# A pair's one-hot rows transposed straight to their places, query casts off GpSimd, later weight slots and a split last tile, in a new hand-written order

## The chip, the cores and the metric

The kernel runs on one core of one Trainium2 chip. The time is device microseconds of one execution. The kernel before was timed three times: 864.74, 865.45 and 865.73 us, median 865.45 us. The engines are named here as the profile names them: PE (TensorE, with PEld for its weight loads), DVE (VectorE), ACT (ScalarE), POOL (GpSimd) and SP (SyncE, which here only issues transfers).

## The reference

Three stages follow one another. The first is attention in which a query sees only the keys of its own cluster, for 2 batches, 8 heads, 768 positions and 64 channels, with 16 clusters; then come two feed-forward blocks.

```python
q_assign = argmax(q_n @ c_n.T)          # one of 16 clusters for each query
k_assign = argmax(k_n @ c_n.T)
mask   = q_assign[:, None] == k_assign[None, :]
scores = where(mask, 0.125 * q @ k.T, -1e9)
x      = softmax(scores) @ v            # heads side by side: 1536 tokens x 512
h = x @ w_in                            # 512 -> 2048
x = where(h > 0, h, exp(min(h, 0)) - 1) @ w_out
return ((x @ w_a) * (x @ w_b)) @ w_out2 # 512 -> 1536 -> 512
```

## The kernel before

Heads are worked off in 8 pairs, each with two halves of three tiles of 128 queries (tile numbers 0 to 5). Every float32 operand is carried as a high part and the rest, so that a product is two or three matmuls. The whole program is one list of words in a string, ORDER, such as `sc:9.4`. A word names a small function and its numbers, and each engine carries out its instructions in the order in which the list issues them. No scheduler moves them.

The words that matter here are these. `lk`, `lq` and `vl` load keys, queries and values. `ka1`, `ka2` and `kbd` make the two parts of the keys; `qa` and `qb` make those of the scaled queries. A third number, where there is one, picks the engine (0 DVE, 1 ACT, 2 POOL). `sm` multiplies a pair with the centroids, `sv`, `st` and `m1` to `m5` turn that into a one-hot row of 16 per head (`oht`). `oh` transposes it on PE for four rows sets at once (two heads, queries and keys), `ohs` scales it on ACT (query rows to 0 or -2^100, key rows to 1 or 0), and `ohd` moves the four pieces by DMA into partitions 64 to 79 of `qb` and `kb`. So the second matmul of a score tile (`sc`, L649, K of 80) adds the mask. `rm` is the negated row maximum on DVE, `ex` the exponential on ACT. Then nearly a third of the tiles (30 of 96) is split into two float16 parts (`hi` on ACT or POOL, `lo` on POOL) and transposed by DMA (`td`); the others are transposed on PE (`tr`) and split from PSUM (`th`, `tl`). `av` is the product with the values, whose parts are `v1` and `v2`; `ra`, `rc`, `rx`, `rb`, `re` and `ev` divide by the row sums.

`wm` issues 8 matmuls on zeros to a scratch bank; the list has 60 of them, all before the second pair's scores. `c0` to `c4` prepare the centroids, with one PE transpose in `c3` (L358).

A weight block of 512 columns comes as int64 pairs that hold float64 (`wl`, 512 KB), and `wa`, `w0` to `w4`, `wh`, `ws` and `wq` turn it into two float32 parts. The block's slot is taken from its pool in `wa` (L829). The feed-forward blocks follow with `h`, `x2`, `ab` and `o`; `oa` adds an `o` tile to the result and, in the last block, sends it out. `o:2.2.1` is the last of them: both its token tiles share one PSUM tile, and `oa` adds and sends them one after the other (L1042 to L1048).

Of the kernel before, what the change touches and what calls it, by code (L numbers as in the profile page):

```python
# [21 lines left out]
P = 128  # L22
# [40 lines left out]

ORDER = """
lk:1.1 wm:0 wm:2 cs:0 cz:0 lq:0.0 ib:0 wm:3 wm:5 lk:0.0 wm:8 lq:1.1 wm:11 vl:0 wm:12 vl:1 md:0 wm:15
kb:1 c0:0 vl:2 wm:18 wm:13 c1:0 vl:3 ka1:1.1 mo:0 c2:0 sb:0 wm:19 wl:0 wm:14 qa:0.2 ce:0 c3:0 wm:28
c4:0 ka2:1.2 wm:29 wm:33 kb:0 wm:35 wm:34 ka1:0.1 qb:0 wm:30 lk:3.0 wm:41 ka2:0.0 wm:10 lq:2.0 wm:46
wm:45 qa:1.2 lk:2.0 wm:47 vr:2 wm:25 qb:1 wm:26 vr:0 wm:56 vr:3 lq:3.0 sm:0.0 vr:1 sm:0.1 sv:0.0.0
vr:5 vr:4 vr:6 wm:22 sv:0.1.0 vr:7 wm:16 st:0 vr:10 wm:38 vr:11 m1:0 wm:20 vr:8 m2:0 wm:40 vr:9 m3:0
wm:57 wm:42 m4:0 wm:48 m5:0 vr:15 wm:31 vr:13 oh:0 wm:55 ohs:0 wm:4 wm:50 wa:0 ohd:0 wm:53 ka1:3.0  # L70
wm:39 vr:12 w0:0 wm:27 vr:14 w1:0 wm:17 kbd:3 w2:0 qa:2.1 vtp:0 wm:43 w3:0 wm:21 wh:0 w4:0 wm:37
ka1:2.1 wm:52 vtd:0 ws:0 wm:58 qa:3.1 kbd:2 sc:0.0 wq:0 sc:0.1 rm:0.0 vbp:0 wm:24 rm:0.1 ka2:2.2
ex:0.0 wl:1 wm:7 wm:36 vbd:0 wm:6 ex:0.1 tr:0.0.0 qb:3 tr:0.0.1 th:0.0.0.1 sc:0.2 th:0.0.1.1 qb:2
tr:0.1.0 sc:1.0 th:0.1.0.1 rm:0.2 vs:0 lq:4.0 wm:1 vs:2 wa:1 rm:1.0 wm:44 lq:5.0 wm:23 ex:0.2
ka2:3.2 wm:32 tl:0.0.0 wm:9 tl:0.1.0 hi:0.2.1 tr:0.1.1 tl:0.0.1 sc:1.1 vs:3 ex:1.0 lk:4.0 sm:1.0
# [178 lines left out]
def clustered_attention_moe_kernel(  # L254
# [842 lines left out]
```

## Time and profile before

| what | value |
|---|---|
| median of 3 | 865.45 us |
| profiled execution | 868.19 us, its span 866.4 us |
| PE busy | 833.2 us (96% of the span) |
| DVE busy | 612.2 us (71%) |
| ACT busy | 412.1 us (48%) |
| POOL busy | 355.5 us (41%) |

The profiled execution is one run by itself, 2.74 us above the median, and 1.8 us of it lie outside its span. PE is busy nearly throughout, but this is an average over stages: in the feed-forward blocks it never waits, in the attention it does. A matmul's end is modelled, so a busy PE is not always a PE at its peak, and where PE's granted clock in the rows is 0.5 it takes twice as long for the same matmuls.

### The profile page before, as it was taken

Reading aid. Unit: us, or ns where it says so; the run is one execution under the profiler, and the core shown is the slowest. Engines: PE = TensorE matmul, PEld = TensorE weight load, DVE = VectorE, ACT = ScalarE, POOL = GpSimd, SP = SyncE. Lnnn points to the kernel's source line nnn. Section 1 sums busy time; section 2 is a strip of 40 time slices with the busy share of each in tenths; the row PEclk is TensorE's granted clock in tenths of the full one; section 3 lists DMA queues with packets and bytes.
Section 4 is the critical chain, followed back from the end, with each engine's and each line's share of the span. In section 5 each row is a group of like instructions: output and inputs, shape, how many; then the busy total and the mean of one; then the engine's idle time right before and its main releaser. Section 6 shows DMA issues by size and latency. Waiting matters only on the chain.

```text
span 866.4 us, 12164 instructions
## 1 busy us (share of the span) xinstructions
PE 833.2 (96%) x4608; PEld 667.4 (77%) x4608; DVE 612.2 (71%) x883; ACT 412.1 (48%) x732; POOL 355.5 (41%) x290
## 2 busy tenths in 40 slices
PE   9898899998898999999999999999999999999997
PEld 8876676676666888888888888888888888888886
DVE  5898898897688986777887876884257872684222
ACT  6587686875677764264264265432122421232120
POOL 4577657674824323444444543342015530451000
PEclk9998999998898999999999999999999999999999
DMA  9445636654323212222222321121002320220102
GB/s 278 111 105 118 137 57 120 135 131 76 74 47 80 67 53 70 97 74 83 88 73 74 91 81 48 54 94 49 0 25 98 96 75 1 74 73 1 49 1 97
DMA packets 65754, 68.32 MB, mean 79 GB/s; under 512 B 49952, under 2 KB 49952, under 8 KB 65696
## 3 DMA queue, kind: packets, MB, share of 16 engines
q1 hardware_dynamic: 65392, 66.86, 29.2%
q10 hardware_dynamic: 304, 0.69, 0.4%
q8 instruction: 36, 0.59, 0.3%
q14 instruction: 22, 0.18, 0.1%
HBM read 48.27 MB, written 3.15 MB: 59 GB/s over the span
## 4 chain that ended last, share of the span: by engine, by line
PE 85%; DVE 7%; POOL 3%; ACT 2%; issue 1%; DMA 0%; ACTq 0%; DVEq 0%; POOLq 0%
PE ab L900 8%; PE ab L901 8%; PE ab L902 8%; PE sc L649 5%; PE h L900 5%; PE h L901 5%; PE h L902 5%; PE x L900 5%; PE x L901 5%; PE x L902 5%; PE tt L701 4%; PE av L760 4%; PE o L902 4%; PE o L900 4%; PE o L901 4%; PE sm L569 3%
## 5 line engine op out<-in xcount | busy, mean ns | idle before, releaser
L657 DVE TENSOR_REDUCE nm<-sc 128x1 f32<-128x768 f32 x96 | 90.2, 948 | 19.9 <-PE sc L649 19.4
L668 ACT ACTIVATE pf<-sc,nm 128x768 f32<-128x768 f32 x96 | 86.5, 902 | 35.2 <-DVE nm L657 31.2
L1002 ACT COPY t0ab<-ab 128x512 f32<-128x512 f32 x36 | 21.1, 587 | 123.1 <-PE ab L902 123.1
L701 PE MATMUL tt<-identf,pf 128*128 128x128 f32 x396 | 65.1, 298 | 14.1 <-DVE pt L710 7.7
L1007 DVE TENSOR_TENSOR t1ab<-ab,t0ab 128x512 f32<-128x512 f32 x36 | 24.8, 688 | 73.2 <-ACT t0ab L1002 73.2
L710 DVE TENSOR_TENSOR pt<-tt,pt 128x384 f16<-128x384 f32 x132 | 68.7, 545 | 8.5 <-ACT pt L705 8.2
L701 PEld LDWEIGHTS tt<-identf,pf 128*128 128x128 f32 x396 | 49.6, 152 | 27.2 <-ACT pf L668 12.0
L649 PE MATMUL sc<-ka,qa 128*128 128x384 f32 x192 | 60.5, 398 | 9.8 <-ACT pf L668 9.8
L705 ACT CAST pt<-tt 128x384 f16<-128x384 f32 x126 | 57.0, 478 | 25.2 <-PE tt L701 24.1
L683 POOL TENSOR_TENSOR phl<-pf,phl 128x768 f16<-128x768 f32 x30 | 50.8, 1693 | 39.9 <-ACT phl L676 37.4
L760 PE MATMUL av<-pt,v 128*64 128x384 f16 x576 | 52.8, 329 | 0.0
L1018 DVE TENSOR_TENSOR gl<-t1ab,gh 128x512 fp32r<-128x512 f32 x36 | 38.4, 1065 | 19.9 <-ACT gh L1013 19.9
L649 PE MATMUL sc<-kb,qb 80*128 80x384 f32 x192 | 52.4, 356 | 0.0
L866 DVE SCALAR_TENSOR_TENSOR wg<-wraw,wg 128x512 f32<-128x512 uint32 x68 | 47.4, 698 | 2.3
L853 DVE SCALAR_TENSOR_TENSOR wf<-wraw,wg 128x512 int32<-128x512 int32 x68 | 47.0, 691 | 2.1
L956 DVE SCALAR_TENSOR_TENSOR t1h<-t0h,h 128x1024 f32<-128x1024 f32 x24 | 29.2, 1215 | 25.2 <-ACT t0h L951 25.1
L649 PEld LDWEIGHTS sc<-ka,qa 128*128 128x128 f32 x192 | 31.6, 203 | 18.9 <-ACT pf L668 13.6
L836 ACT ACTIVATE wg<-wraw 128x512 f32<-128x512 f32 x68 | 45.1, 667 | 1.6 <-DMA wraw<-in_w_a_dram 0.9
L760 PEld LDWEIGHTS <-v 128*64 128x64 f16 x576 | 31.3, 110 | 16.2 <-issue 4.9
L971 DVE TENSOR_TENSOR gl<-t1h,gh 128x1024 fp32r<-128x1024 f32 x24 | 36.1, 1504 | 5.4 <-ACT gh L964 5.4
L841 DVE TENSOR_SCALAR wg<-wg 128x512 f32<-128x512 f32 x68 | 38.4, 565 | 2.1 <-ACT wg L836 1.9
L846 DVE TENSOR_SCALAR wg<-wg 128x512 int32<-128x512 int32 x68 | 38.0, 559 | 2.1
(387 smaller groups left out, 2356.8 us busy)
## 6 DMA issues: line engine op xcount, KB each, us to landing
wraw<-in_w_out_dram SPq DMA_DIRECT2D x28, 512.0 KB, 3.2
wraw<-in_w_in_dram SPq DMA_DIRECT2D x16, 512.0 KB, 3.6
wraw<-in_w_a_dram SPq DMA_DIRECT2D x12, 512.0 KB, 3.5
wraw<-in_w_b_dram SPq DMA_DIRECT2D x12, 512.0 KB, 3.5
rawq<-in_qt_dram SPq DMA_DIRECT2D x30, 192.0 KB, 3.7
acc<-in_v_dram SPq DMA_DIRECT2D x4, 768.0 KB, 9.5
rawk<-in_kt_dram SPq DMA_DIRECT2D x15, 192.0 KB, 3.7
kb<-ka SPq DMA_DIRECT2D x14, 192.0 KB, 3.1
```

The lines of the kernel that those rows point to most:

```text
L649: nc.tensor.matmul(s[:, j, :HALF], a[:, qs], b[:, j * HALF : (j + 1) * HALF], start=i == 0, stop=i == 1,)
L657: nc.vector.reduce_max(out=nm, in_=st[g][f"sc{t}"][:, :, :HALF], axis=AX.XY, negate=True)
L668: nc.scalar.activation(pf.rearrange("p (a b) -> p a b", a=2), st[g].pop(f"sc{t}")[:, :, :HALF], AF.Exp, bias=st[g].pop(f"nm{t}"), accum_ou ...
L683: nc.gpsimd.tensor_sub(phl[:, S:], st[g].pop(f"pf{t}"), phl[:, :S])
L701: nc.tensor.transpose(tt[:, k * P : (k + 1) * P], pf[:, o : o + P], identf)
L705: (nc.vector.tensor_copy, nc.scalar.copy)[e](next(parts_of(g, t, u)), st[g][f"tt{t}{u}"])
L710: nc.vector.tensor_sub(lo, st[g].pop(f"tt{t}{u}"), hi)
L760: nc.tensor.matmul(pairs[j]["av"][x * 64 : (x + 1) * 64].rearrange("p (a q) -> p a q", a=3), st[2 * j + x][("v1", "v2")[vi]][:, kt_, :], s ...
L866: nc.vector.scalar_tensor_tensor(out=g, in0=raws.pop(n)[:, :, 0].bitcast(U32), scalar=2.0 ** -52, in1=g, op0=ALU.mult, op1=ALU.mult,)
L900: nc.tensor.matmul(ps, lhi, rhi, start=first, stop=False)
L901: nc.tensor.matmul(ps, lhi, rlo, start=False, stop=False)
L902: nc.tensor.matmul(ps, llo, rhi, start=False, stop=last)
```

## The change

ORDER is written anew from end to end (2394 words before, 2401 now). Four things in the functions go with it.

- The first pair has no `oh:0`, `ohs:0` and `ohd:0` any more. `ot:n` transposes the one-hot rows of one of its four sets on PE straight to partitions 64 to 79 of a PSUM tile, and `oe:n` scales or copies them to their place in `qb` (DVE) or `kb` (ACT). The other seven pairs keep the old way.
- A weight block's slot is taken in `wh` instead of `wa`, so `wa` to `w4` of its first piece no longer stand behind the block that had the slot.
- The last `o` tile is two PSUM tiles, `o` and `o2`, with `oa` and `ob` behind them.
- Engines of single words: `qa` is never on POOL now (seven of its sixteen were there; ACT has six of them and DVE one, and the two that DVE had are on ACT too). `v1` and `v2` are never on DVE (five and five were; `v1` goes to POOL four times and to ACT once, `v2` to POOL). `hi` goes from ACT to POOL for twelve tiles and the other way for two, six more `ka1` are on POOL, and two fewer `re` and one fewer `sv` on DVE.

```diff
 ORDER = """
-lk:1.1 wm:0 wm:2 cs:0 cz:0 lq:0.0 ib:0 wm:3 wm:5 lk:0.0 wm:8 lq:1.1 wm:11 vl:0 wm:12 vl:1 md:0 wm:15
...
+lk:1.1 lk:0.0 wm:0 wm:2 lq:1.1 cz:0 lq:0.0 ib:0 wm:4 wm:6 cs:0 wm:7 wm:10 vl:2 wm:11 wl:0 mo:0 wm:15
...
+wm:46 wm:48 c2:0 lq:2.0 vr:9 wm:24 wm:53 vr:10 wm:55 lq:3.0 vr:8 wm:17 vr:11 c3:0 wm:42 wa:0 c4:0
...
+    @op
+    def ot(n):
+        o = box["ot", n] = small([P, S], f"ot_{n}", BF16)
+        for t in range(NT):
+            nc.tensor.transpose(
+                o[64:80, t * P : (t + 1) * P], pairs[0]["oht"][:, t, n * C : (n + 1) * C], identb
+            )
+
+    @op
+    def oe(n):
+        o = box.pop(("ot", n))[64:80]
+        if n < 2:
+            nc.vector.tensor_scalar(
+                operand(n, "qb")[64:80], o, BIG, -BIG, op0=ALU.mult, op1=ALU.add
+            )
+        else:
+            nc.scalar.copy(operand(n - 2, "kb")[64:80], o)
+
     @op
     def ohd(j):
         for x in range(2):
             for n, name in ((x, "qb"), (2 + x, "kb")):
-                (nc.scalar if j == 0 and n > 1 else nc.sync).dma_start(
+                nc.sync.dma_start(
...
     @op
     def wa(n):
-        i, a = divmod(n, 4)
-        if a == 0:
-            wt[i] = tuple(
-                take(pools[f"w{i % 4}"], f"w{i % 4}{x}", [P, 4, BLK], F32R, f"w{i}{x}")
-                for x in "hl"
-            )
         p = raw_pool(n)
...
     @op
     def wh(n):
         i, a = divmod(n, 4)
+        if a == 0:
+            wt[i] = tuple(
+                take(pools[f"w{i % 4}"], f"w{i % 4}{x}", [P, 4, BLK], F32R, f"w{i}{x}")
+                for x in "hl"
+            )
         nc.scalar.copy(wt[i][0][:, a, :], wgf[n][1].bitcast(F32))
...
+    @op
+    def o2(blk, c, jp):
+        ps = hold["o2"] = mlp_psum(f"o2_{blk}_{c}_{jp}")
+        o_tile(ps[:, 0, :], blk, c, 2 * jp + 1)
...
+    @op
+    def ob(blk, c, jp):
+        t = c * (CH // P) + 2 * jp + 1
+        a = by_token[:, t : t + 1, :]
+        nc.vector.tensor_add(a, hold.pop("o2")[:, :1], a)
+        send(a, t)
```

In the new list 27 `wm` (216 matmuls) stand ahead of `c3` and 32 ahead of the first `sm`; before it was 12 (96 matmuls) and 26. Ahead of the first score tile it is 46, before 47.

What stands on DVE around the first row maxima, before (`vm` to `vdg` are the values' scale, `nm` the maxima of score tiles, `qb` the second pair's queries):

```order
L439 TENSOR_REDUCE vm<-vps 16x1
...
L451 TENSOR_SCALAR vdg<-identf,ve 16x16 x2
L657 TENSOR_REDUCE nm_0_684<-sc_0_673 128x1
L657 TENSOR_REDUCE nm_0_696<-sc_0_679 128x1
L465 COPY vsc<-vbc 128x32
L468 COPY vback<-vsc 64x8 x2
L480 SCALAR_TENSOR_TENSOR qb_737<-rawq_405,qa_669 64x768
L480 SCALAR_TENSOR_TENSOR qb_751<-rawq_345,qa_609 64x768
L657 TENSOR_REDUCE nm_0_763<-sc_0_745 128x1
```

And now:

```order
L441 TENSOR_REDUCE vm<-vps 16x1
...
L453 TENSOR_SCALAR vdg<-identf,ve 16x16 x2
L649 TENSOR_SCALAR qb_328<-ot_616 16x768
L467 COPY vsc<-vbc 128x32
L470 COPY vback<-vsc 64x8 x2
L482 SCALAR_TENSOR_TENSOR qb_683<-rawq_367,qa_633 64x768
L679 TENSOR_REDUCE nm_0_693<-sc_0_678 128x1
L679 TENSOR_REDUCE nm_0_707<-sc_0_688 128x1
L649 TENSOR_SCALAR qb_346<-ot_699 16x768
L482 SCALAR_TENSOR_TENSOR qb_750<-rawq_396,qa_673 64x768
L679 TENSOR_REDUCE nm_0_766<-sc_0_745 128x1
```

The first maximum now stands behind the `oe` copy, the copies of the values' scale and one `qb`.

What stands on DVE between the fifth and the sixth pair, before (the numbers in a name are the head and a running number; `v1_10` and `v1_11` are the sixth pair's values):

```order
L480 SCALAR_TENSOR_TENSOR qb_12_2753<-rawq_12_2419,qa_12_2719 64x768
...
L657 TENSOR_REDUCE nm5_9_2800<-sc5_9_2758 128x1
L480 SCALAR_TENSOR_TENSOR qb_13_2806<-rawq_13_2431,qa_13_2783 64x768
L492 CAST v1_10_2821<-acc_66 128x384
L492 CAST v1_11_2827<-acc_66 128x384
L657 TENSOR_REDUCE nm0_10_2835<-sc0_10_2816 128x1
L657 TENSOR_REDUCE nm1_10_2852<-sc1_10_2829 128x1
```

And now:

```order
L482 SCALAR_TENSOR_TENSOR qb_12_2791<-rawq_12_2418,qa_12_2727 64x768
L679 TENSOR_REDUCE nm5_9_2805<-sc5_9_2784 128x1
...
L679 TENSOR_REDUCE nm0_10_2834<-sc0_10_2800 128x1
...
L679 TENSOR_REDUCE nm1_10_2881<-sc1_10_2859 128x1
L732 TENSOR_TENSOR pt1_9_2809<-tt40_9_2868,pt1_9_2809 128x384
L482 SCALAR_TENSOR_TENSOR qb_13_2897<-rawq_13_2435,qa_13_2798 64x768
```

The two casts have left DVE, and the maxima of the sixth pair come ahead of `qb_13`.

What stands on POOL in the same place, before:

```order
L519 CAST ka_12_2679<-rawk_12_2514 64x768
L526 TENSOR_TENSOR ka_12_2679<-rawk_12_2514,ka_12_2679 64x768
L543 TENSOR_SCALAR qa_12_2719<-rawq_12_2419 128x768
L676 CAST phl5_8_2733<-pf5_8_2709 128x768
L683 TENSOR_TENSOR phl5_8_2733<-pf5_8_2709,phl5_8_2733 128x768
L543 TENSOR_SCALAR qa_13_2783<-rawq_13_2431 128x768
L526 TENSOR_TENSOR ka_13_2798<-rawk_13_2504,ka_13_2798 64x768
L683 TENSOR_TENSOR phl5_9_2838<-pf5_9_2810,phl5_9_2838 128x768
```

And now:

```order
L494 CAST v1_10_2675<-acc_66 128x384
L499 TENSOR_TENSOR v2_10_2687<-acc_66,v1_10_2675 128x384
L494 CAST v1_11_2702<-acc_66 128x384
L499 TENSOR_TENSOR v2_11_2707<-acc_66,v1_11_2702 128x384
L521 CAST ka_12_2725<-rawk_12_2363 64x768
L528 TENSOR_TENSOR ka_12_2725<-rawk_12_2363,ka_12_2725 64x768
L698 CAST phl5_8_2759<-pf5_8_2737 128x768
L705 TENSOR_TENSOR phl5_8_2759<-pf5_8_2737,phl5_8_2759 128x768
L521 CAST ka_13_2807<-rawk_13_2541 64x768
L528 TENSOR_TENSOR ka_13_2807<-rawk_13_2541,ka_13_2807 64x768
L698 CAST phl5_9_2854<-pf5_9_2832 128x768
```

The two query casts are gone from POOL; the values' parts, one key cast and one `hi` cast have come.

## Rows read from the trace of the kernel before

**Rows 1.** Windows: stretch, its us, busy us of each engine, granted clock, DMA

```profile
31.80:293.20 261.40, 235.77 (x1704) 178.35 (x1702) 223.54 (x355) 188.74 (x399) 159.42 (x131) 0.93 0.48 101
293.20:861.90 568.70, 568.63 (x2505) 463.21 (x2503) 368.64 (x493) 203.38 (x288) 184.42 (x125) 1.00 0.19 62
```

**Rows 2.** Windows: four stretches of the attention

```profile
65.00:75.00 10.00, 6.43 (x30) 5.62 (x30) 8.47 (x13) 7.35 (x17) 9.44 (x8) 0.66 0.74 181
95.00:110.00 15.00, 12.69 (x71) 8.86 (x67) 12.24 (x18) 9.93 (x23) 5.28 (x5) 0.89 0.66 145
...
185.00:205.00 20.00, 15.97 (x97) 12.15 (x97) 15.46 (x22) 10.46 (x23) 16.39 (x13) 0.83 0.60 143
215.00:245.00 30.00, 25.70 (x167) 19.63 (x168) 20.53 (x32) 19.65 (x42) 18.46 (x13) 0.83 0.36 69
```

**Rows 3.** Timeline: start us, us, instruction, idle before it; between 185 and 200

```profile
190.99 0.95 DVE L480 SCALAR_TENSOR_TENSOR qb<-rawq,qa 64x768 fp32r<-64x768 f32 x1 [1.85 <-POOL qa L543]
191.04 2.59 POOL L526 TENSOR_TENSOR ka<-rawk,ka 64x768 fp32r<-64x768 f32 x1
...
191.87 3.69 DVE L492 CAST v<-acc 128x384 f16<-128x384 f32 x2
...
197.97 0.87 PE L701 MATMUL tt<-identf,pf 128*128 128x128 f32 x3 [3.33 <-DVE pt L710]
```

**Rows 4.** Timeline of the first 33 us, PE and DVE

```profile
1.18 7.90 PE L405 MATMUL warm_ps<-warm 128*128 128x128 bf16 x96 [1.18 <-DVE eps L309]
...
9.03 6.42 PE L405 MATMUL warm_ps<-warm 128*128 128x128 bf16 x112
...
15.26 0.36 PE L569 MATMUL sm<-qa,cq 128*64 128x384 f32 x1
...
20.18 0.58 PE L583 MATMUL tp<-identf,sim 64*128 64x64 f32 x6
...
23.18 0.56 DVE L615 TENSOR_TENSOR oht<-tp,mx 128x384 bf16<-128x384 f32 x1
...
29.47 0.28 PE L434 MATMUL vps<-identf,vmax 128*16 128x128 f32 x1 [1.79 <-ACT junk L427]
...
30.69 1.49 DVE L451 TENSOR_SCALAR vdg<-identf,ve 16x16 f32<-16x16 f32 x2
...
31.79 0.60 PE L649 MATMUL sc<-ka,qa 128*128 128x384 f32 x2
```

**Rows 5.** Groups of DVE from 31.8 to 293.2: busy, mean ns, idle before

```profile
L657 DVE TENSOR_REDUCE nm<-sc 128x1 f32<-128x768 f32 x96 | 90.2, 948 | 19.9 <-PE sc L649 19.4
...
L492 DVE CAST v<-acc 128x384 f16<-128x384 f32 x5 | 6.1, 1239 | 1.2 <-PE av L760 1.2
...
L497 DVE TENSOR_TENSOR v<-acc,v 128x384 f16<-128x384 f32 x5 | 2.9, 588 | 0.1
...
L746 DVE COPY rb<-rbp 128x384 f32<-128x384 f32 x4 | 2.2, 545 | 0.0
L543 DVE TENSOR_SCALAR qa<-rawq 128x768 fp32r<-128x768 f32 x2 | 1.1, 550 | 0.0
```

**Rows 6.** Line 492, the values' casts: minimum, median and maximum ns

```profile
L492 DVE CAST v<-acc x5: 320/1757/1976, 121.9 to 245.5; 128x384 f16<-128x384 f32 x5
```

**Rows 7.** Groups of POOL and ACT from 31.8 to 293.2

```profile
L683 POOL TENSOR_TENSOR phl<-pf,phl 128x768 f16<-128x768 f32 x30 | 50.8, 1693 | 39.9 <-ACT phl L676 37.4 <-issue 1.1
L526 POOL TENSOR_TENSOR ka<-rawk,ka 64x768 fp32r<-64x768 f32 x14 | 28.0, 2001 | 2.1 <-ACT ka L519 1.1
L676 POOL CAST phl<-pf 128x768 f16<-128x768 f32 x16 | 14.4, 903 | 24.5 <-ACT pf L668 21.9 <-issue 2.1 <-POOL ka L526 0.4
...
L543 POOL TENSOR_SCALAR qa<-rawq 128x768 fp32r<-128x768 f32 x5 | 10.6, 2126 | 1.7 <-PE sc L649 1.7
...
L676 ACT CAST phl<-pf 128x768 f16<-128x768 f32 x14 | 11.7, 837 | 0.2
```

**Rows 8.** Timeline of the last 5 us, DVE

```profile
861.87 1.29 DVE L1044 TENSOR_TENSOR acc<-o,acc 128x512 f32<-128x512 f32 x2 [4.22 <-PE o L902]
```

More of the change, by code (lines that the diff above doesn't have):

```diff
@@ L70 @@
[L70 to L75, printed above, removed]
@@ new lines @@
+rm:1.2 wm:9 th:1.0.1.1 tr:1.1.0 w2:1 tr:1.1.1 ex:1.2 sc:0.3 w3:1 w4:1 wm:36 wh:1 sc:0.4 th:1.1.0.1
+tl:1.0.1 hi:1.2.2 ra:0.0 wm:34 rm:0.3 th:1.1.1.1 ws:1 sm:1.1 rm:0.4 ex:0.3 wq:1 wm:32 tl:1.1.0
+sv:1.1.1 sc:0.5 tl:1.1.1 ex:0.4 lo:1.2 wl:2 rc:0.0 st:1 rm:0.5 ka1:4.1 sc:1.3 m1:1 rx:0.0 qa:4.1
+td:1.2 m2:1 ka2:4.2 tr:0.3.0 tr:0.3.1 ex:0.5 m3:1 wm:35 kbd:4 m4:1 wm:43 th:0.3.0.1 sc:1.4 m5:1
+hi:0.5.2 th:0.3.1.1 tl:0.3.0 oh:1 wa:2 lo:0.5 tl:0.3.1 rb:0.0 ohs:1 rm:1.3 tr:0.4.0 re:0.0.1
+tr:0.4.1 ohd:1 rm:1.4 th:0.4.0.1 ex:1.3 th:0.4.1.0 tl:0.4.0 ex:1.4 tr:1.3.0 qb:4 td:0.5 tr:1.3.1
@@ L250 @@
+pl:2.2.2 o:2.1.0 bs:2.2.3 pr:2.2.3 ph:2.2.3 pl:2.2.3 o:2.1.1 oa:2.1.0 o:2.2.0 oa:2.1.1 o:2.2.1
+oa:2.2.0 o2:2.2.1 oa:2.2.1 ob:2.2.1
 """
@@ L1020, in clustered_attention_moe_kernel, with last, o_tile @@
     by_token = acc.rearrange("p a b -> p (a b)").rearrange("p (t m) -> p t m", m=DM)
+    def last(blk, c, jp):
+        return (blk, c, jp) == (NB2 - 1, NCH - 1, 1)
+    def o_tile(ps, blk, c, jt):
+        w, (ph, pl) = wt[NW1 + 3 * blk + 2], hold["p", blk, c]
+        js = slice(jt * P, (jt + 1) * P)
+        for ft in range(NFT):
+            mm3(ps, ph[:, ft, js], pl[:, ft, js], w[0][:, ft, :], w[1][:, ft, :],
+                ft == 0, ft == NFT - 1)
     @op
@@ L1024, in o, with send @@
         ps = hold["o", blk, c, jp] = mlp_psum(f"o{blk}_{c}_{jp}")
-        w, (ph, pl) = wt[NW1 + 3 * blk + 2], hold["p", blk, c]
-        for j in range(2):
-            js = slice((2 * jp + j) * P, (2 * jp + j + 1) * P)
-            for ft in range(NFT):
-                mm3(ps[:, j, :], ph[:, ft, js], pl[:, ft, js], w[0][:, ft, :], w[1][:, ft, :],
-                    ft == 0, ft == NFT - 1)
+        for j in range(1 if last(blk, c, jp) else 2):
+            o_tile(ps[:, j, :], blk, c, 2 * jp + j)
+    @op
+    def o2(blk, c, jp):
+        ps = hold["o2"] = mlp_psum(f"o2_{blk}_{c}_{jp}")
+        o_tile(ps[:, 0, :], blk, c, 2 * jp + 1)
+    def send(a, t):
+        nc.sync.dma_start(
+            out=out[t * P : (t + a.shape[1]) * P, :].rearrange("(j p) m -> p j m", p=P), in_=a
+        )
     @op
@@ L1035, in oa @@
         t0 = c * (CH // P) + 2 * jp
-        a = by_token[:, t0 : t0 + 2, :]
+        n = 1 if last(blk, c, jp) else 2
+        a = by_token[:, t0 : t0 + n, :]
         if blk == 0:
             nc.vector.tensor_copy(a, ps)
-        elif blk < NB2 - 1:
-            nc.vector.tensor_add(a, ps, a)
-        else:
-            n = 1 if t0 == NTOK // P - 2 else 2
-            for j in range(0, 2, n):
-                nc.vector.tensor_add(a[:, j : j + n], ps[:, j : j + n], a[:, j : j + n])
-                nc.sync.dma_start(
-                    out=out[(t0 + j) * P : (t0 + j + n) * P, :].rearrange("(j p) m -> p j m", p=P),
-                    in_=a[:, j : j + n],
-                )
+        else:
+            nc.vector.tensor_add(a, ps[:, :n], a)
+        if blk == NB2 - 1:
+            send(a, t0)
+    @op
[4 more added lines that the diff above has]
+        send(a, t)
     for word in ORDER.split():
```

354 lines of the change are left out of this document (176 added, 178 removed).

## The prediction, made blind

> **What bounds the kernel now.** I read the windows first, cut at the first score tile (31.8 us), at the first feed-forward matmul (293.2) and at the last one's end (861.9). The reader is to see in [rows 1] that from 293.2 on PE is busy 568.63 of 568.70 us at full clock. Nothing that this change does to other engines can shorten that part, unless it makes PE wait. Ahead of it lie 261.4 us of attention in which PE is busy 235.8, so idle 25.6, at a granted clock of 0.93, and DVE is busy 223.5 (86%). Next come windows inside that stretch [rows 2]: the idle time comes in lumps, and in each lump or behind it the clock falls to about half. The groups [rows 5] say what DVE does there: 90 of its 223 us are row maxima, which wait 19.9 us for PE's scores, so PE and DVE take turns at being late. The timeline of one lump [rows 3] shows how: a query cast of 2.1 us on POOL holds a `qb` on DVE for 1.85 us, then DVE runs two value casts for 3.69 us while POOL runs a subtraction, the maxima come behind them, and PE sits idle 3.33 us. At the front [rows 4] PE is bound by its own warm-up matmuls; at the end [rows 8] two additions run one behind the other.
>
> **The start, term 0.** The transposed one-hot rows no longer pass through a transfer, but what counts is when PE reaches the first score. 96 warm-up matmuls start at 1.18; 112 more take 6.42 us, 57 ns each [rows 4]. Now 216 stand ahead of the centroids' transpose: the first 96 end at about 8.9, 120 more take 6.8, so that transpose comes at 15.7 instead of 8.9. Then 0.3 for it and 40 warm-ups (2.3), which hide the six small DVE copies: the centroid products begin at 18.3, 3.0 us later than 15.26. From there to the next transposes (`tp`) it was 4.9 us, 16 warm-ups included; there are 16 again, so they come at 23.2. The one-hot ends 3.56 us behind them (20.18 to 23.74 before), at 26.8, beside 72 warm-ups that keep PE to 27.7. The values' transpose, 29.47 before because it waited for ACT, can go at 27.7: ACT's 16 value maxima no longer stand behind two transfers on its queue. From it to the end of `vdg` it was 2.7 us (32.18 less 29.47); two `ot` groups and 8 warm-ups hide beside that. Then the small product and 16 warm-ups, 1.3 us: the first score at 31.7, against 31.79. So the wait that goes is eaten by the warm-ups put in its place. Behind it DVE now has an `oe` (a PSUM read of 768 elements, bounded by a row maximum's 0.948, [rows 5], and by 0.3, the shortest cast of half as many [rows 6]; I take 0.95, the nearer form), the scale copies and a `qb` ahead of the first maximum, but one `qb` fewer behind it. I take 0, with bounds of 2 earlier and 3 later.
>
> **The attention, term -8.6.** DVE loses, in this stretch, five `v1` (6.1 us by their rows), five `v2` (2.9), two `qa` (1.1), two `re` (1.1) and one `sv` (0.55), and gains one `oe` (0.95; the other lies ahead of the stretch): 10.8 less of 223.5 [rows 5]. What remains on it has the same shapes. POOL loses five `qa` at 2.13 (10.6), and two key subtractions (4.0) and one weight piece that now lie ahead of the first score; it gains ten `hi` net at 0.90 (9.0), five `v2` and three `v1` (some 6, estimated from `hi` with half the elements and `lo` with half) and five `ka1` (some 4): by this about 2 more of 159.4, still 62% [rows 7]. ACT loses ten `hi` at 0.84 and gains eight `qa` of about the same length; it stays near 72%, not the bound. PE gains 18 small transposes and nothing else.
>
> How much of DVE's 10.8 reaches the end? Upper bound: three of the four lumps have an instruction that leaves in their chain (a DVE `qa` and `v2` at 95 to 110, POOL's `qa` and DVE's `v1` at 185 to 205, POOL's `qa` at 215 to 245). Their idle time is 2.3 + 4.0 + 4.3 and their lost clock at most 0.11 x 15 + 0.17 x 20 + 0.17 x 30 = 10.2, in all 20.8 [rows 2]. Lower bound: nothing, if PE's turns grow by what DVE's shrink. Between them lie two sums. With the durations as they stand DVE gives 10.8. But a `v1` cast takes 0.32 at least and 1.76 in the median [rows 6], so 4.6 of its 6.1 us are time in which DVE did nothing itself; if such waits only move to the next DVE instruction that meets POOL, DVE gives 6.2. I take the middle, 8.6, because POOL is as busy as before, while the waits that stood straight ahead of the maxima are gone.
>
> The Trainium skill (SBUF — State Buffer, Who interferes with whom) has a rule for this: a DVE cast in its fast mode and a GpSimd instruction share a port, and whichever came first blocks the other for its whole length; a row maximum never waits there. The trace agrees with it (0.32 against 1.76 us, with a POOL subtraction beside it). By the rule the casts' waits go altogether, and the term would be nearer to 10.8.
>
> **The weights, term 0.** Slots taken later let four small groups of the first piece start earlier. They matter where weights are late, and PE never waits behind 293.2. A loss would need a weight part to come after its matmul; PE's 0.07 us of idle there says that the order had no such place before, and the new list has the pieces about as far ahead of their blocks.
>
> **The end, term -0.65.** The two additions take 1.29 us behind the last matmul [rows 8]. With a tile each, the first runs beside the other tile's 12 matmuls, so one is left: half of 1.29. Its transfer is issued earlier by as much and finds no other in flight, so nothing is late in its place. Bounds 0 and -1.3.
>
> **Sum.** 0 - 8.6 - 0.65 = -9.25. The profiled execution took 868.19, of which 866.4 is its span; it would be 858.9. The median lay 2.74 below it, so I predict 865.45 - 9.25 = 856.2.
>
> **Rivals.**
> *All three lumps go.* Then 20.8 + 0.65 are saved: 844.0. For it speaks that each has a removed instruction in its chain, and that clock lost behind a wait comes back with it; against it, that lumps at 65 to 75 (weight work on DVE) show the same form without any of these.
> *PE is the bound and DVE's gain is hidden.* Only the end is left: 864.8. For it: maxima wait 19.9 us for scores [rows 5] and PE is busy 90%. Against it: PE's busy time has stretches at half clock in it, behind waits on DVE.
> *POOL takes the place of ACT as the late one: slower.* Twelve `hi` that ran on ACT (0.84) now queue on POOL, each ahead of its own `lo` (1.69), and behind whatever is there, up to a key subtraction of 2.0 [rows 7]. The DMA transposition waits for `lo`, the loads and one-hot transfers queue behind it on SP, and `av` on PE for its result. A tile can be late by 0.07 + 2.0; if all twelve pass it on it is 24.8 us. The change is slower from 4.5 tiles on (9.25 / 2.07). With half of them it is 12.4 - 9.25: 868.6. For it: POOL's `lo` waits 39.9 us for its `hi` in sum, so the chain is a late one already. Against it: the wait is POOL's own, which has 38% idle, and a tile's transposed parts are used a half pair later.
> *The start is as late as the extra warm-ups* (3.0 us at the products, nothing won back): 859.2, inside the forecast's own range of 851 to 862.
>
> **Chances.** Forecast with the late start 0.60, all lumps 0.13, hidden gain 0.12, POOL late 0.15. A measurement of this kernel can tell 0.2%, 1.7 us, from no change. Faster: the first two, 0.73, plus little of the hidden case, 0.74; same: 0.11; slower: 0.15. The range of 846 to 867 leaves out the lower part of the second case and about half of the last.
>
> **What would show it.** Right: first score at 31 to 33 with its centroid products near 18.3; no `v1` over 0.6 us anywhere on DVE, since there is none; DVE busy some 11 us less between first score and first feed-forward matmul, and that stretch about 253 us long; PE idle there under 20 us and the granted clock above 0.94; from there 568.7 us unchanged; one addition of 0.64 behind the last matmul. Wrong: the stretch as long as before with DVE idle in it instead of busy (PE or POOL was the bound); POOL named as releaser of ACT's or PE's waits, or SP waiting longer for `lo`; or PE idle anywhere behind the first feed-forward matmul, which would be the weights.

## The result and the profile after

The changed kernel takes 843.34 us (median of 4; 842.81 to 846.78), the kernel before 865.1 beside it: ratio 0.9757, 95% interval 0.9729 to 0.9785, faster by 21.8 us. Forecast were 856.2 us and a range of 846 to 867, so the direction was right and the size was not: the time lies below the range. Timed again in two later sets of runs, its medians were 843.01 and 843.71. Three executions that took far longer than the others of their kernel (953.94 us of `weights_apart`, the only one of it with a trace, 1014.39 of `weights_bunched` and 1629.31 of the kernel before) are left out of every time below.

The profiled execution took 843.85 us, its span 842.1. The windows, cut as before at the first score, the first feed-forward matmul and the end of the last matmul (columns as in [rows 1]):

```profile
32.15:270.10 237.95, 226.30 (x1725) 166.97 (x1723) 215.15 (x341) 185.35 (x397) 160.16 (x145) 1.00 0.54 107
270.10:838.43 568.33, 568.33 (x2502) 462.94 (x2500) 374.07 (x491) 202.28 (x285) 184.00 (x125) 1.00 0.19 62
```

Against [rows 1] the feed-forward part is the same to 0.4 us. The attention is 23.4 us shorter in this pair of executions; the one before lay 2.74 us above its median and this one 0.51, so in the medians it is some 21.2. PE's idle time in it falls from 25.6 to 11.7 us (14.0), and its busy time by 9.5 us although its records hold 21 matmuls more: the granted clock is 1.00, where it was 0.93. DVE is busy 8.4 us less, POOL 0.7 us more. The four stretches that had the lumps [rows 2] now read:

```profile
65.00:75.00 10.00, 10.00 (x75) 7.63 (x74) 9.29 (x17) 7.43 (x17) 6.35 (x7) 1.00 0.80 172
95.00:110.00 15.00, 14.96 (x106) 10.82 (x103) 13.97 (x24) 11.50 (x26) 9.25 (x9) 1.00 0.68 142
185.00:205.00 20.00, 19.55 (x135) 13.49 (x133) 18.10 (x31) 15.40 (x35) 12.82 (x13) 1.00 0.75 135
215.00:245.00 30.00, 29.52 (x223) 21.36 (x223) 25.47 (x42) 22.98 (x50) 17.13 (x17) 1.00 0.43 77
```

All four lumps are gone (0.0, 0.04, 0.45 and 0.48 us of PE's idle time are left), the one at 65 to 75 too, from which no instruction was taken. By groups (busy, mean ns, idle before), DVE from 32.15 to 270.1:

```profile
L679 DVE TENSOR_REDUCE nm<-sc 128x1 f32<-128x768 f32 x96 | 90.9, 950 | 14.3 <-PE sc L671 13.6
...
L482 DVE SCALAR_TENSOR_TENSOR qb<-rawq,qa 64x768 fp32r<-64x768 f32 x14 | 17.2, 1239 | 0.1
```

`qb` no longer waits (1.85 us in one place in [rows 3]), and the maxima wait 14.3 us for scores instead of 19.9 [rows 5]. POOL in the same stretch:

```profile
L705 POOL TENSOR_TENSOR phl<-pf,phl 128x768 f16<-128x768 f32 x30 | 50.9, 1696 | 4.7 <-issue 1.9 <-ACT phl L698 0.9
L698 POOL CAST phl<-pf 128x768 f16<-128x768 f32 x26 | 23.5, 903 | 43.9 <-ACT pf L690 42.9 <-POOL ka L528 0.7
```

Its subtractions wait 4.7 us instead of 39.9 [rows 7]; the wait stands before its `hi` casts now. The front, PE alone, to be laid beside [rows 4]:

```profile
1.20 14.85 PE L407 MATMUL warm_ps<-warm 128*128 128x128 bf16 x216 [1.20 <-DVE eps L311]
...
15.88 0.28 PE L360 MATMUL cps<-identf,cn 128*128 128x128 f32 x1
...
18.20 0.37 PE L571 MATMUL sm<-qa,cq 128*64 128x384 f32 x1
...
23.12 0.58 PE L585 MATMUL tp<-identf,sim 64*128 64x64 f32 x6
...
27.67 0.27 PE L436 MATMUL vps<-identf,vmax 128*16 128x128 f32 x1
...
32.15 0.59 PE L671 MATMUL sc<-ka,qa 128*128 128x384 f32 x2
```

The two later traces of the same kernel have the first score at 31.21 and 32.33 us, so a difference of 1 us at the start lies within what it moves by itself.

And the end, one addition where [rows 8] had two; the span ends 3.67 us behind the last matmul instead of 4.50:

```profile
838.47 0.69 DVE L1087 TENSOR_TENSOR acc<-o,acc 128x512 f32<-128x512 f32 x1 [2.03 <-PE o L923]
```

### The profile page after: what moved, and what is told of

Read it like the earlier page. It is cut to its first block, busy times and chain, and to the rows that moved or that the text cites. A ratio compares the mean times of both kernels' runs of the same rounds, so it can differ in the third digit from the quotient of the medians.

```text
span 842.1 us, 12217 instructions
## 1 busy us (share of the span) xinstructions
PE 823.9 (98%) x4626; PEld 656.1 (78%) x4626; DVE 609.5 (72%) x871; ACT 408.3 (48%) x730; POOL 357.5 (42%) x307
## 4 chain that ended last, share of the span: by engine, by line
PE 90%; DVE 4%; POOL 3%; ACT 2%; issue 2%; POOLq 0%; ACTq 0%; DVEq 0%
PE ab L923 8%; PE ab L922 8%; PE ab L921 8%; PE sc L671 6%; PE h L921 5%; PE h L923 5%; PE h L922 5%; PE x L923 5%; PE x L921 5%; PE x L922 5%; PE av L782 4%; PE o L923 4%; PE o L921 4%; PE o L922 4%; PE tt L723 4%; PE sm L571 4%
## 5 line engine op out<-in xcount | busy, mean ns | idle before, releaser
L679 DVE TENSOR_REDUCE nm<-sc 128x1 f32<-128x768 f32 x96 | 90.9, 950 | 14.3 <-PE sc L671 13.6
L671 PE MATMUL sc<-ka,qa 128*128 128x384 f32 x192 | 58.2, 384 | 7.1 <-ACT pf L690 6.5
L723 PE MATMUL tt<-identf,pf 128*128 128x128 f32 x396 | 60.3, 277 | 4.1 <-DVE pt L732 2.0
L723 PEld LDWEIGHTS tt<-identf,pf 128*128 128x128 f32 x396 | 45.7, 140 | 15.1 <-issue 4.3
L869 DVE SCALAR_TENSOR_TENSOR wf<-wraw,wg 128x512 int32<-128x512 int32 x68 | 51.2, 753 | 1.9
L882 DVE SCALAR_TENSOR_TENSOR wg<-wraw,wg 128x512 f32<-128x512 uint32 x68 | 49.7, 731 | 1.8
L671 PE MATMUL sc<-kb,qb 80*128 80x384 f32 x192 | 49.5, 339 | 0.0
L1039 DVE TENSOR_TENSOR gl<-t1ab,gh 128x512 fp32r<-128x512 f32 x36 | 33.8, 940 | 18.8 <-ACT gh L1034 18.6
L671 PEld LDWEIGHTS sc<-ka,qa 128*128 128x128 f32 x192 | 28.8, 189 | 19.8 <-ACT pf L690 13.6
L862 DVE TENSOR_SCALAR wg<-wg 128x512 int32<-128x512 int32 x68 | 41.8, 615 | 2.1
L698 POOL CAST phl<-pf 128x768 f16<-128x768 f32 x26 | 23.5, 903 | 43.9 <-ACT pf L690 42.9
```

The lines of the kernel that those rows point to most:

```text
L671: nc.tensor.matmul(s[:, j, :HALF], a[:, qs], b[:, j * HALF : (j + 1) * HALF], start=i == 0, stop=i == 1,)
L679: nc.vector.reduce_max(out=nm, in_=st[g][f"sc{t}"][:, :, :HALF], axis=AX.XY, negate=True)
L723: nc.tensor.transpose(tt[:, k * P : (k + 1) * P], pf[:, o : o + P], identf)
L869: nc.vector.scalar_tensor_tensor(out=f, in0=raws[n][:, :, 1], scalar=-0x40000000, in1=g, op0=ALU.bitwise_and, op1=ALU.bitwise_or,)
```

## The experiments

The kernel before runs beside every set: its medians there lie between 863.4 and 866.9 us, and its single runs go with the granted clock (862.15 us at 0.985, 869.31 at 0.978). Where no other kernel is named, the changed kernel's 843.0 to 843.7 is what a time is held against. Line numbers of the experiments' kernels lie 8 to 10 below those of the kernel that they were made from (2 below in the two kernels with stalls). The diffs show single words picked out of ORDER, with ... for what lies between.

### Order against engines

Two kernels split the change: the new order with the old engines, and the old order with the new engines.

```diff
 # old_engines: the changed order, 64 words behind the first score
-hi:0.5.2 ... ka1:6.1 ... qa:9.1 ... v1:10.2 ... v2:13.2
+hi:0.5.1 ... ka1:6.2 ... qa:9.2 ... v1:10.0 ... v2:13.0
 # new_engines: the order before, the same words the other way
```

Among the 64 are twelve `th`, six each way between DVE and ACT, which the list of engines ahead of the prediction does not name. What is called the order here is all of the change but these words: the first pair's new way, the later slots and the split last tile are in it, the last with 0.83 us.

> The changed kernel's order word for word, but behind the first score every cast, subtraction and copy of the attention (64 of them: hi, v1, v2, qa, ka1, th, re, sv) runs on the engine that it had before. Before 865.1 us, changed 843.3. Theory 'engines' (the gain is that value and query casts no longer stand on DVE and POOL ahead of row maxima): 860 to 866, the clock of the attention back near 0.93 and PE idle near 25 us. Rival 'places' (the gain is where the words stand, whichever engine runs them): 842 to 847. Rival 'fit' (an order and its engines only go together): above 866.

Measured: 854.33 us (854.14 to 855.88), before 866.22 beside it.

> The mirror image: the order of the kernel before word for word, with the 64 engines of the changed one behind the first score; start and tail as before. Theory 'engines': 844 to 850. Rival 'places': 862 to 867, no change. Rival 'fit': above 867.

Measured: 858.0 us (857.25 to 859.16). So the order alone gives 11.9 us and the engines alone 8.2, together 20.1 of some 22. Neither pure theory holds, and "fit" is not needed at this level: the two nearly add. The windows of the old order with the new engines:

```profile
31.80:282.40 250.60, 227.91 (x1698) 169.64 (x1697) 215.11 (x336) 183.62 (x396) 165.43 (x148) 0.98 0.49 105
...
65.00:75.00 10.00, 7.32 (x37) 6.38 (x37) 9.02 (x14) 7.44 (x18) 9.53 (x8) 0.83 0.78 192
95.00:110.00 15.00, 13.07 (x86) 9.07 (x81) 10.82 (x18) 12.77 (x28) 7.39 (x8) 1.00 0.66 145
185.00:205.00 20.00, 18.60 (x135) 12.82 (x133) 16.81 (x24) 14.07 (x32) 15.06 (x15) 1.00 0.76 163
215.00:245.00 30.00, 27.32 (x205) 20.10 (x203) 23.12 (x37) 19.75 (x45) 19.20 (x19) 1.00 0.36 68
...
260.00:265.00 5.00, 4.94 (x24) 4.33 (x26) 4.38 (x10) 4.43 (x11) 4.06 (x4) 0.66 0.26 98
```

and of the new order with the old engines:

```profile
31.80:280.60 248.80, 231.16 (x1732) 170.32 (x1730) 223.93 (x358) 187.97 (x400) 150.60 (x127) 0.99 0.51 103
...
65.00:75.00 10.00, 10.00 (x74) 7.59 (x73) 9.11 (x17) 7.79 (x17) 6.13 (x6) 1.00 0.75 177
95.00:110.00 15.00, 14.95 (x96) 10.45 (x93) 13.12 (x23) 12.18 (x27) 7.61 (x7) 1.00 0.78 156
185.00:205.00 20.00, 16.87 (x100) 12.40 (x99) 15.89 (x27) 12.78 (x29) 13.63 (x10) 0.91 0.69 155
215.00:245.00 30.00, 29.07 (x210) 21.83 (x208) 26.79 (x45) 22.96 (x48) 13.07 (x10) 0.94 0.41 71
```

The engines restore the clock in the three later stretches, though not at 260 to 265 (0.66), and leave the lump at 65 to 75. The order takes that lump away and, although no instruction in them changes its engine, nearly all idle time at 95 to 110 and at 215 to 245 as well (0.05 and 0.93 us are left); it leaves 3.1 us at 185 to 205. DVE is as busy in the whole attention as before (223.9 us), and the attention is 12.6 us shorter: DVE's load does not set it.

### Which of the engines

```diff
 # v_as_before
-v1:10.2 ... v2:13.2 ... v1:14.2
+v1:10.0 ... v2:13.0 ... v1:14.0
 # q_as_before (in the changed kernel) and, the other way in the kernel before, q_only
-qa:6.1 qa:8.1 qa:9.1 qa:12.1 qa:13.1 qa:14.1 qa:15.1
+qa:6.0 qa:8.0 qa:9.2 qa:12.2 qa:13.2 qa:14.2 qa:15.2
```

> The changed kernel with only the value casts and subtractions (v1, v2; 15 words) on their former engines, so that DVE has 5 v1 and 5 v2 again. Theory 'engines': DVE busy 9 us more in the attention, 849 to 854, one or two stretches at half clock. Rival 'places': 842.5 to 845. The prediction's own price for this part was 4.6 to 9 us, without the clock.

Measured: 846.72 us (845.43 to 846.84), 3.0 to 3.7 above the changed kernel.

> The changed kernel with only the query casts behind the first score (7 words) on their former engines: 5 on POOL at about 2.1 us each, 2 on DVE. Theory 'engines': qb on DVE waits for POOL again, 847 to 853, with idle lumps of PE near those qb. Rival 'places': 842.5 to 845.

Measured: 853.47 us (852.29 to 853.66), 10 us above the changed kernel.

> The kernel before with only its seven later query casts moved, five from POOL and two from DVE, to ACT; order and all other engines kept. All 64 engines together gave 8.2 us there; undoing these seven in the changed kernel cost 10. Theory 'the queries carry the engines' share': 856 to 860, the wait of qb for POOL (5.5 us) gone. Rival 'the value casts do': 863 to 867.

Measured: 854.03 us (853.4 to 859.19), before 864.13 beside it. So seven query casts are worth 10 us in either order, about the whole share of the engines. In the old order the trace shows the way that I had named, the wait of `qb` on DVE for POOL. Groups of DVE in the attention, of the kernel before and then of `q_only`:

```profile
L480 DVE SCALAR_TENSOR_TENSOR qb<-rawq,qa 64x768 fp32r<-64x768 f32 x14 | 17.5, 1262 | 5.5 <-POOL qa L543 5.5
```

```profile
L472 DVE SCALAR_TENSOR_TENSOR qb<-rawq,qa 64x768 fp32r<-64x768 f32 x14 | 16.1, 1162 | 0.9 <-ACT qa L533 0.9
```

ACT's waits for row maxima fall with it, from 31.0 to 22.2 us. How much of the 10 us comes by this wait alone is not separated. In the new order the way is another: in the changed kernel with those casts on POOL (`q_as_before`), `qb` waits 0.1 us in sum. What waits there is what stands behind the cast on POOL's own queue (timeline, POOL, then PE and ACT):

```profile
182.70 2.13 POOL L535 TENSOR_SCALAR qa<-rawq 128x768 fp32r<-128x768 f32 x1
...
184.79 0.82 POOL L511 CAST ka<-rawk 64x768 fp32r<-64x768 f32 x1
...
185.69 1.81 POOL L518 TENSOR_TENSOR ka<-rawk,ka 64x768 fp32r<-64x768 f32 x1
...
187.56 1.43 POOL L688 CAST phl<-pf 128x768 f16<-128x768 f32 x1
...
189.50 1.65 PE L753 MATMUL rbp<-identf,rx 128*128 128x128 f32 x6 [2.81 <-POOL rx L743]
...
191.08 0.90 ACT L680 ACTIVATE pf<-sc,nm 128x768 f32<-128x768 f32 x1 [4.99 <-POOL phl L695]
```

The exponential waits 4.99 us for a probability buffer that POOL's subtraction still reads, and PE 2.81 us for the row factors that POOL spreads; PE's granted clock is 0.50 from 190 to 195. Over the attention ACT's waits for POOL's subtraction are 14.3 us here and 7.1 in the changed kernel.

In `v_as_before` the value casts are on DVE again, in the new order; one line for all five:

```profile
L484 DVE CAST v<-acc x5: 351/359/360, 111.9 to 234.3; 128x384 f16<-128x384 f32 x5
```

The same instructions took 1757 ns in the median before [rows 6]. When they start here no POOL instruction is running; the three long ones before (two from 191.87 us on and one at 245.51) start while a POOL subtraction runs. With all 64 old engines in the new order (`old_engines`) four of the five are short, and one, started while a key subtraction runs on POOL, takes 1.78 us:

```profile
L484 DVE CAST v<-acc x5: 343/384/1779, 114.1 to 243.9; 128x384 f16<-128x384 f32 x5
```

The Trainium skill (SBUF — State Buffer, Who interferes with whom) says that issue order and not the shape of an operation decides which of DVE and GpSimd blocks; these traces agree, 0.36 us against 1.76 for the same shape on the same engine. The prediction had the rule, and took these waits to go only with the casts' engine.

### The casts on POOL

```diff
-hi:0.5.2 hi:1.2.2 ... hi:5.5.1 ... hi:13.5.2
+hi:0.5.1 hi:1.2.1 ... hi:5.5.2 ... hi:13.5.1
```

> The changed kernel with the 12 probability casts that moved to POOL back on ACT (and two back on POOL). The prediction's rival 'POOL is late' would make this faster than the changed kernel, up to 12 us: under 842. Theory 'POOL has room': 842 to 847, since POOL's subtraction then waits for ACT again while the transposed parts are used half a pair later.

Measured: 842.12 us (841.78 to 844.42), 0.9 to 1.6 us below the changed kernel. POOL is busy 149.7 us then (160.2 with the casts), and ACT's waits for its subtraction are 2.6 us (7.1). So these casts cost little, in the direction of the rival of a late POOL and far below the 12.4 us that the prediction put on half of them. In this order POOL is late through the query casts that leave it.

### The places of the weight work

```diff
 # weights_apart: the kernel before, pieces 1 to 5 by a rule of mine
-w0:2 w1:2 ex:1.5 kbd:5 w2:2 tr:1.3.0 tr:1.3.1 w3:2 tr:1.4.0 wh:2 sc:2.0 w4:2
+w0:2 w1:2 ... rm:2.0 w2:2 wh:2 ... rm:2.1 ws:2 w3:2 w4:2 ... rm:2.2 wq:2 wl:3
 # weights_bunched: the changed kernel
-w0:2 th:2.1.1.1 td:2.2 w1:2 ... rm:3.2 ... w2:2 ex:3.2 sc:2.3 w3:2 w4:2
+rm:3.2 ... w0:2 w1:2 w2:2 w3:2 w4:2 ex:3.2 sc:2.3
 # weights_as_after: the kernel before, pieces 2 and 3 where the changed one has them
-wa:2 w0:2 w1:2 ... w2:2 ... w3:2 ... wh:2 ... w4:2 ... ws:2 ... wq:2 ... rm:2.0
+rm:0.5 wa:2 ... rm:3.1 w0:2 w1:2 ... rm:3.2 w2:2 w3:2 w4:2 wh:2 ... rm:2.3 ws:2 wq:2
 # weights_as_before: the changed kernel, pieces 2 to 5 where the kernel before has them
-rm:3.1 ... w0:2 ... w1:2 ... rm:3.2 ... w2:2 ... w3:2 w4:2 ... wh:2 rm:2.3
+rm:1.5 wa:2 w0:2 w1:2 w2:2 w3:2 wh:2 w4:2 ws:2 wq:2 ... rm:2.0
```

> The kernel before with all its engines; only the words of weight pieces 1 to 5 moved (w2 to w4, wh, ws, wq and one load behind them), so that no more than three of a piece's five DVE words stand between two row maxima. The order alone, engines kept, gave 11.9 us. Theory 'weights in a row': the idle lumps at 65 to 70 (3.6 us) and 265 (2.2) and the clock behind them go: 855 to 859. Rival 'spread': the order's gain comes from many small places, this one gives 0 to 2 us: 863 to 867. Rival 'late weights': PE waits behind the first feed-forward matmul, over 868.

Measured: 878.66 us (876.35 to 881.08), slower by 1.3% (0.7 to 1.8). Why is not shown.

> The mirror image in the changed kernel: w0 to w4 of pieces 1 to 5 each in one row (2.7 us of DVE) at the place of w2, engines kept. Theory 'weights in a row': up to five new lumps of 1 to 3 us, 846 to 852, the clock below full in one or two places. Rival 'spread': 842 to 845.

Measured: 849.01 us (848.31 to 849.19), 5.3 to 6.0 above the changed kernel. The granted clock falls to 0.69 at 115 to 120; it reads 0.66 at 30 to 35 too, ahead of the moved words.

> The kernel before with its engines; only weight pieces 2 and 3 (w0 to w4, wa, wh, ws, wq, one load) stand behind the same row maxima as in the changed kernel: piece 2 four maxima later, piece 3 spread over eight. Spreading by a rule of my own had made it slower, so this takes the changed kernel's own places. Theory 'places of the weights': the lump at 65 to 75 goes (3.6 us idle and 3.4 of clock): 857 to 861. Rival 'fit' (a place is right only with the words around it): 864 to 872, a lump elsewhere instead.

Measured: 873.64 us (870.84 to 876.42), slower by 1.0%. The edit brought a wait of its own, and decides nothing on rows of weight words:

```profile
55.15 0.66 ACT L827 ACTIVATE wg<-wraw 128x512 f32<-128x512 f32 x1 [2.67 <-DMA wraw<-in_w_in_dram]
```

Piece 2's load was issued at 51.16 us, and `wa` on ACT starts 4.0 us behind it; in the changed kernel it is 7.4 us (48.74 to 56.10). The exponentials stand behind `wa`, and PE waited 5.4 us for them.

> The changed kernel with weight pieces 2 to 5 behind the row maxima behind which they stood before (four or five of DVE's words in a row each), engines kept. Bunched at places of their own they cost about 6 us. Theory 'places of the weights': 847 to 853, with a lump near 65. Rival: 842 to 845.

Measured: 852.03 us (851.6 to 856.59) against 843.01 for the changed kernel on the same chip: 9.0 us. Here no load is late. DVE and, in the line of L713, PE:

```profile
61.07 0.96 DVE L669 TENSOR_REDUCE nm<-sc 128x1 f32<-128x768 f32 x1
61.94 0.42 DVE L847 TENSOR_SCALAR wg<-wg 128x512 f32<-128x512 f32 x1
...
64.05 0.69 DVE L872 SCALAR_TENSOR_TENSOR wg<-wraw,wg 128x512 f32<-128x512 uint32 x1
...
65.35 0.52 PE L713 MATMUL tt<-identf,pf 128*128 128x128 f32 x3 [2.05 <-DVE pt L722]
65.59 0.95 DVE L669 TENSOR_REDUCE nm<-sc 128x1 f32<-128x768 f32 x1
```

Five weight words in a row hold DVE for 2.7 us; the evictions and the next maximum (4.5 us behind the last one) come after them, PE waits 2.05 us, and the granted clock is 0.66 from 65 to 70. So in the new order the old places of the weight work cost 9.0 us. That the new places bring as much of the order's 11.9 us is not shown: bunching at places of their own costs 5.3 to 6.0 too, and both trials in the old order came out slower.

> The changed kernel unchanged, on the chip of these runs, as the measure for the others: 842 to 845.

Measured: 843.01 us (842.86 to 843.8).

### What a stall costs

```diff
+    def ds(n):
+        for _ in range(n):
+            nc.vector.reduce_max(out=stall_out, in_=warm, axis=AX.X)
...
-rm:5.0 ... rm:7.3 ... rm:9.3 ... rm:11.3
+ds:3 rm:5.0 ... ds:3 rm:7.3 ... ds:3 rm:9.3 ... ds:3 rm:11.3
 # stall_long: ds:6
```

> The changed kernel with three extra row maxima of the 128x512 bf16 warm tile on DVE straight ahead of four score maxima (5.0, 7.3, 9.3, 11.3): about 0.6 us each by the row maximum of 768 elements, 1.8 us a place, 7 us in all; result unused. Theory 'clock' (a lump of over 2 us is followed by a stretch at half clock, so order decides through few lumps): where a lump stays short nothing more than its length comes, 846 to 850. Rival 'slack' (DVE and PE take turns, short delays vanish): 843 to 845.

Measured: 848.59 us (848.45 to 851.72). The extra work is 4 x 2.12 = 8.5 us of DVE; the whole kernel is 5.6 us above 843.01. The trace, of the longest of the four runs, shows the clock falling behind short stalls too, against the theory's clause on short lumps, here behind a wait of PE of 1.77 us (0.57 from 150 to 155):

```profile
151.36 1.01 PE L669 MATMUL sc<-ka,qa 128*128 128x384 f32 x2 [1.77 <-ACT pf L688]
```

> The same with six at each of the four places, about 3.6 us a place, 14 us in all. Theory 'clock': idle lumps of 2 to 3.5 us on PE, behind them the clock at about half for 5 us, each place costs more than its 3.6 us: 858 to 868 and the clock of the attention under 0.96. Rival 'length alone': 852 to 857 with the clock at 1.00.

Measured: 865.25 us (860.47 to 867.9, 10 runs). The extra work is 4 x 4.28 = 17.1 us, and the kernel is 22.2 us above 843.01. The attention from 31.8 us on, first with the short stalls and then with the long ones, and what follows it with the long ones, as windows:

```profile
31.80:281.20 249.40, 233.78 (x1719) 170.62 (x1718) 221.56 (x351) 185.88 (x397) 158.20 (x144) 0.97 0.50 102
```

```profile
31.80:295.20 263.40, 239.40 (x1733) 175.93 (x1730) 230.00 (x367) 186.21 (x397) 158.51 (x145) 0.94 0.47 97
295.20:863.90 568.70, 565.08 (x2501) 462.87 (x2499) 375.20 (x491) 202.09 (x285) 184.57 (x125) 1.00 0.20 62
```

From the first feed-forward matmul to the end of the span it is 568.7 us in both kernels with stalls and 572.0 in the changed kernel, 3.3 us less for a reason that no trace shows. So the stalls cost the attention some 8.9 and 25.5 us: twice the work, about three times the price.

One of the long stalls as a timeline, PE and DVE:

```profile
191.31 0.52 PE L669 MATMUL sc<-kb,qb 80*128 80x384 f32 x2
...
192.36 4.28 DVE L325 TENSOR_REDUCE stall_out<-warm 128x1 f32<-128x512 bf16 x6
...
198.65 1.01 PE L669 MATMUL sc<-ka,qa 128*128 128x384 f32 x2 [3.80 <-ACT pf L688]
199.45 0.84 PE L669 MATMUL sc<-kb,qb 80*128 80x384 f32 x2
```

DVE is held for 4.28 us, PE waits 3.80, and the same two matmuls that took 0.52 us before take 0.84 behind it. In this trace the attention, from its first score at 32.19, is 25.1 us longer than the changed kernel's; about half of that is idle time (24.0 against 11.7) and half is busy time at the lower clock.

### The start

```diff
 # oh_by_transfer
-ot:0 ... ot:2 ... oe:2 oe:0 ... ot:1 ... ot:3 ... oe:1 ... oe:3
+m5:0 oh:0 ohs:0 ohd:0
 # fewer_warm, fewer_warm_again: seven words of eight warm-ups ahead of c3 taken out
-wm:20 wm:46 wm:48 wm:24 wm:53 wm:55 wm:17
```

> The changed kernel with the first pair's one-hot rows sent to their places by four transfers again (oh, ohs, ohd behind m5) and without the 24 small transposes and four evictions. Theory 'the start is PE's queue': the rows land before the first score all the same, 842 to 845, no difference that can be measured. Rival 'the transfer was the wait': first score 1 us later or more, 845 to 848.

Measured: 845.09 us (844.63 to 846.19), 1.4 to 2.1 above the changed kernel. ACT's scaling and the transfers stand ahead of its value maxima again, the values' transpose waits for them, and the first score comes at 33.64, 1.3 to 2.4 us later than in the three traces of the changed kernel:

```profile
29.59 0.28 PE L426 MATMUL vps<-identf,vmax 128*16 128x128 f32 x1 [0.85 <-ACT junk L419]
...
33.64 0.59 PE L661 MATMUL sc<-ka,qa 128*128 128x384 f32 x2
```

> The changed kernel without 7 of the 27 groups of warm-up matmuls that stand ahead of the centroids' transpose (56 matmuls of 57 ns, 3.2 us); the normalised centroids are ready at 11.6 in the trace, the transpose runs at 15.9. Theory 'PE's own queue sets the start': first score 3 us earlier, 839.5 to 841. Rival 'the attention is paced by DVE and POOL': PE starts earlier and waits more behind, 842 to 844. Rival 'clock': with fewer matmuls at the start the first products run at half clock, over 843.

Measured: 842.29 us (840.21 to 843.75): first score at 28.9, 2.3 to 3.5 us earlier, but two of the four runs (843.71 and 843.75) give it back. The trace is of one of them, and the clock falls twice in it, at 85 to 95 and at 250 to 260 us.

> The changed kernel without the 56 warm-up matmuls, timed again: 840 to 841 where the clock stays whole, 843.7 where one stretch falls to half.

Measured: 841.54 us (840.25 to 843.76): the clock falls in three of the four runs here, and the one at 1.00 throughout took 840.25.

### Both edits together

The version has the edit of `fewer_warm` and that of `hi_as_before`, both shown above.

> The changed kernel without the 56 warm-ups and with the 14 probability casts on their former engines. If both gains stand and add (3 us and 0 to 1): 838.5 to 840.5 with the clock at 1.00. Rival 'fit': the attention that starts 3 us earlier meets its weights and loads in other places, a stretch falls to half clock, 841 to 845.

Measured: 839.59 us (838.97 to 841.1, 6 runs).

> The changed kernel unchanged, on the same chip beside it, as the measure for the version with both edits: 842.5 to 844.

Measured: 843.71 us (842.9 to 846.72, 6 runs). Every run of the version with both edits is below every run of the changed kernel beside it, by 4.1 us in the medians; it beats both kernels. Its first score stands at 28.35 (timeline):

```profile
28.35 0.60 PE L661 MATMUL sc<-ka,qa 128*128 128x384 f32 x2
```

The attention behind it is 0.85 us shorter than the changed kernel's 237.95 (windows):

```profile
28.30:265.40 237.10, 226.19 (x1727) 166.90 (x1724) 215.30 (x341) 192.46 (x408) 150.30 (x135) 1.00 0.54 108
```

## Why the prediction was wrong

**The start, 0: right.** First score at 32.15, worked out 31.7; products at 18.20 (18.3), transposes at 23.12 (23.2), values' transpose at 27.67 (27.7). The first score moves by 1.1 us between traces of this kernel, so a closer agreement would say nothing. That the wait which goes is eaten by the warm-ups in its place is shown from both sides: with the transfers back it comes 1.3 us later or more, with 56 warm-ups fewer 2.3 us earlier or more.

**The attention, -8.6: the step that failed.** Measured: -23.4 in the profiled pair, some -21.2 in the medians. The step is "How much of DVE's 10.8 reaches the end?". It took the term from the busy time of the instructions that leave DVE, and held the rest of the order at nothing. (The middle of its two sums, 10.8 and 6.2, is 8.5.) DVE's load fell by 8.4 us, not 10.8, and it is not what sets the stretch: with the load unchanged the new order still gives 11.9. What the sum had no term for is that order: the prediction saw the lump at 65 to 75 and its cause, weight work on DVE, used it as an argument against the larger case because none of its instructions was removed, and did not look where the new list puts those words. In the new order, their old places cost 9.0 us.

**The engines: near, by luck.** They give 8.2 us in the old order and 11.0 in the new, beside the 8.6. But 9.0 of the 10.8 were value casts and subtractions, which measured 3.0 to 3.7 in the new order; the query casts, priced at 1.1 us for the two on DVE and at nothing for the five on POOL, measured 10. The prediction had seen their wait [rows 3] and used it in the upper bound alone. In the old order it goes when they leave POOL; in the new one, back on POOL, they hold up what stands behind them there.

**The clock.** The prediction had its loss only as an upper bound for three lumps. It came back whole: 9.5 us of PE's busy time. A lump is paid twice, as idle time and as a stretch at the lower clock behind it; in the long stalls the two are about equal. The upper bound of 20.8 was passed, by 2.6 us in the profiled pair and by 0.4 in the medians, since it counted three lumps; the clock fell in five places, the fifth at 265 to 280 with 2.3 us of idle time in it.

**The weights, 0: wrong in what it looked at.** PE never waits for weights behind the first feed-forward matmul, as said. But their price was not there: it was DVE's time in the attention. What the later slots alone bring was not tried.

**The end, -0.65:** -0.83 measured.

**The rivals.** "All three lumps go" gave 844.0, and the time is 843.3; its mechanism is half of it. Engines alone take the idle time from 4.0 to 1.4 us at 185 to 205, from 4.3 to 2.7 at 215 to 245 and only from 2.3 to 1.9 at 95 to 110, and the clock's loss in all three. But the order alone empties two of these lumps with no instruction removed, and the rest of the sum came from lumps that this rival left standing. "PE is the bound" fell: PE's busy time itself shrank. "POOL is late" came out small: its sign, ACT waiting for POOL, did show (3.2 us before, 7.1 now), but the 12 casts cost 0.9 to 1.6 us. "The start is late" fell with the first score.

Left open: how the order's 11.9 us split. One of the two trials in the old order brought a late load of its own, and why the other is slower is not shown.

## What to carry to other kernels

In a program whose order is written out, price a new order by what stands between two instructions of the engine that others wait for (here the row maxima), and not by the sums of the engines: DVE's sum could stay as it was and 12 us went. Look at both sides of an instruction in a slow engine's queue: five casts of 2.1 us on POOL and two on DVE cost 10 us in either order, in one beside waits for their results, in the other beside waits for what stood behind them. And where a stall is followed by a lower clock, long waits cost more than their length: 1.5 us for each us of held DVE with the long stalls here, about 1.0 with the short ones. Long runs of side work are worth pulling apart, but the places have to be tried: here a rule for it made the old order slower.

## What the runs showed of the hardware

- A scaled cast of 128x768 from float32 to fp32r takes 2.13 us on POOL, 0.84 on ACT and 0.55 on DVE; a cast of the same size to float16 takes 0.90 on POOL and 0.84 on ACT. I had not expected the first ratio beside the second.
- The same 128x384 cast on DVE took 0.32 to 0.41 us where no POOL instruction ran on for more than 0.2 us behind its start, and 1.76 to 1.98 where a POOL subtraction did. Before, two of five were short; with the order alone changed, four.
- The granted clock fell behind single waits of PE of 1.77 us (0.57 from 150 to 155), 2.05 us (0.66 from 65 to 70) and 3.80 us (0.52 from 200 to 205), while in the changed kernel stretches of 5 us with up to 1.58 us of idle time stayed at 1.00.
- Evictions of one-hot rows from partitions 64 to 79 of PSUM (16x768, bfloat16) take 0.96 us on DVE and 0.79 on ACT, about what 128 partitions of that length take (0.95 and 0.84 to 0.90).
